# Fences on every load of the opening: banded attention followed by four experts, one core

## The chip, the cores and the metric

The kernel runs on one core of one Trainium2 chip. The metric is the device time of one execution in microseconds (us). A profile of one execution is shown beside the times; its times count from the start of its span. PE is TensorE, DVE VectorE, ACT ScalarE, POOL GpSimd, SP SyncE, whose queue issues nearly all DMAs.

## What is computed

Attention over 4 batches, 8 heads, 576 positions and 64 columns, where a query sees 32 keys at most (heads 4 to 7: every fourth key back to 128), and then a layer of 4 experts on the 2304 x 512 result, weighted by given probabilities:

```
scores = where(mask, scale * q @ k.T, -1e9)
attn = exp(scores - max); attn = attn / (sum(attn) + 1e-9)
x = (attn @ v) as 2304 x 512
p = domain_probs / (sum(domain_probs) + 1e-9)
for e in range(4):
    h = relu(x @ w1[e]); out += p[:, e] * (h @ w2[e])      # w1[e] 512x1024, w2[e] 1024x512
```

All is float32. The products of the experts are made of a high and a low part of each operand, three matmuls for one.

## The kernel before

**Attention in steps.** A step is two groups of 192 queries; there are 24. Step m goes through stages: `s_qk` (scores `sc`, 48 small matmuls, L300), `s_max` (masked maxima `sm`, `nm` on VectorE, L314), `s_sub` (GpSimd, L328), `s_exp` (ScalarE, L335), `s_sum` (row sums `su`, `rc` on VectorE, L341 to L345), `s_norm` (GpSimd, L350), `s_tr` (transpose `pt` on PE, copy `pts` on ScalarE, L361 to L365), `s_av` (products `po` with the V tile, 48 small matmuls, L381, and a copy of each of the two results to `xr`, L398 on VectorE or L400 on ScalarE).

**Experts in units.** A unit is 256 of an expert's 1024 inner columns: 16 units, each for three blocks of 768 tokens; the first two units of the first block come with attention. `fetch_w1` and `fetch_w2` load a unit's W1 (tile `r`, tag r1) and W2 (tag r2); ScalarE makes the high part and VectorE or GpSimd the low one (`split`, L127 and L130: `g1h`, `g1l`, `w2h`, `w2l`, of x `xh`, `xl`). The product with W1 is `product` (L431, results m1x, m1y), then relu (`hh`, `hl`, L449 to L455), the product with W2 is `mm2` (L535), and VectorE adds it to `acc` (L539, L544). `x_sums` (L227) are differences of x for a Strassen-like scheme.

**Rounds.** The program is written in rounds n (L851). Round n does `s_qk` of the step whose place is n, `s_max` and the later stages of the steps before; `s_av` of a step comes 3 rounds after its `s_qk`. Steps 0 to 4 have places 0 to 4, steps 5 to 9 have 8 to 12, step 10 has 16. START is 7, OPEN is 15. From round START on, pieces of the experts are taken between the stages; up to START, PE is given dummy matmuls (`wt`, L775). So `po` of step 4 is in round 7, of step 8 in round 14; `sc` of step 9 is in round 12.

**Loads.** At the start of each round, and in rounds 3 and 4 once more behind `s_max` (mid = 1), `load_ready` goes down the list `loads` and issues what is ready. A load goes to SP's queue, which is worked off in order, so a load that waits holds all behind it. A buffer's reuse makes a load wait by itself (`QKB` 3 buffers for q and k, `VB` 4 for V, 2 for W1, 1 for raw W2). A fence is a memset of one column of the tile on VectorE ahead of its DMA: the DMA waits for the memset, and the memset stands in VectorE's order where the round begins. In the kernel before, fences stand on W1 of units 0 and 2, on q of steps 5 and 10, and on V of steps 2, 3 and 4:

```
ready["w1"] = lambda u: n >= (needed[0] + 1, 0, OPEN - 2)[u]
waits = {needed[0] + 1: needed[0] + 1, needed[1] + 1: OPEN}
fenced = range(2, needed[0] + 1)
```

(needed is 4 and 9.) The rest of the opening's loads go as soon as the list and the buffers let them.

Of the kernel before, what the change touches and what calls it, by code (L numbers as in the profile page):

```python
# [23 lines left out]
QKB = 3  # L24
VB = 4
# [23 lines left out]
def kernel(  # L49
# [11 lines left out]
    nc = tc.nc  # L61
# [37 lines left out]
    w2_op = {}  # L99
    raw1 = {}  # L100
    raw2 = {}

    def fetch_w1(u, part=0):
        e, s = divmod(u % NU, FPE)
        if not part:
            raw1[u] = wp.tile([128, 4, FU], F32, tag="r1", name="r1", bufs=2)
            if u in (0, 2):
                nc.vector.memset(raw1[u][:, 0, :1], 0.0)
        c = slice(part, 4 if u or part else 2)
        src = w1[e, :, s * FU:(s + 1) * FU].rearrange("(c p) f -> p c f", p=128)  # L110
        nc.sync.dma_start(out=raw1[u][:, c], in_=src[:, c])

    def fetch_w2(u):
        e, s = divmod(u % NU, FPE)
        r = wp.tile([128, 2, DM], F32, tag="r2", name="r2")
        nc.sync.dma_start(
            out=r, in_=w2[e, s * FU:(s + 1) * FU, :].rearrange("(c p) d -> p c d", p=128)
        )
        raw2[u] = r
# [124 lines left out]
    def attention(ap, xrp, pa):  # L244
# [125 lines left out]
        def s_av(n, gs):  # L370
            ts_ = st.pop(n)
            v_s = v_of.pop(n)
            po = [pa.tile([128, 512], F32, tag="pa", name="po") for _ in gs]
            for i in range(GS):
                for half in range(2):
                    for k in range(len(gs)):
                        rows = slice(KB * k, KB * (k + 1))
                        for j in range(2):
                            c = i * 128 + 64 * (j ^ k) + QB * half
                            o = i * SB + QB * half  # L380
                            nc.tensor.matmul(  # L381
                                po[k][64 * j:64 * j + 64, o:o + QB],
                                v_s[rows, j, 2 * i + half, :], ts_[rows, c:c + QB],
                                start=True, stop=True,
                            )

            for k, (b, p, gi) in enumerate(gs):
                x = x_raw(b)[:, p, :]
                src = po[k][:, :GW]
                if p < NP // 2:  # L390
                    nt = GW // DILATION
                    dst = x.rearrange("q (r t) -> q r t", r=DILATION)
                    dst = dst[:, :, gi * nt:(gi + 1) * nt]
                    src = src.rearrange("q (t r) -> q r t", r=DILATION)
                else:
                    dst = x[:, gi * GW:(gi + 1) * GW]
                if 0 < n < 3:
                    nc.vector.tensor_copy(out=dst, in_=src)  # L398
                else:
                    nc.scalar.activation(out=dst, in_=src, func=AF.Copy)  # L400
# [258 lines left out]
    with tc.manual_schedule():  # L659
# [15 lines left out]
        s_av, s_tr, s_max = (stages[0][i][0] for i in (1, 2, 3))  # L675
# [112 lines left out]
        START = done(*dil(0, 0, 2))  # L788
        OPEN = done(*dil(1, 0))
        when = {}  # L790
        for n, i, names in (
# [8 lines left out]
        first_x = []  # L800
        qk_done = av_done = 0
        shares = []
        ready = {"w2": lambda u: u < 1 or (u - 1, 1) in w2_op and (u < 2 or n >= OPEN)}
        ready["w1"] = lambda u: n >= (needed[0] + 1, 0, OPEN - 2)[u]
        waits = {needed[0] + 1: needed[0] + 1, needed[1] + 1: OPEN}
        ready["qk"] = lambda m: m < qk_done + QKB and n >= waits.get(m, 0)
        fenced = range(2, needed[0] + 1)
        ready["v"] = lambda m: (
            m < av_done + VB
            and (m <= needed[1] or m <= qk_done)  # L810
            and (m not in fenced or (n, mid) >= ((3, 1), (4, 1))[m > 3])
        )

        def load(what, m):
            if what == "qk":
                load_qk(steps[m], nc.sync if m else nc.scalar, m in waits)
            elif what == "v":
                load_v(m, steps[m], m in fenced)
            elif what == "masks":
                load_masks()  # L820
            elif what == "rest":
                fetch_w1(m, 2)
            elif what == "probs":
                shares.append(load_probs())
            else:
                (fetch_w1 if what == "w1" else fetch_w2)(m)

        loads = [
# [4 lines left out]
        ]  # L833
        for m in range(needed[1] + 1, len(steps)):
            loads += [("qk", m), ("v", m)]
# [2 lines left out]
        def load_ready():  # L838
            at = 0
            while at < len(loads):  # L840
                what, m = loads[at]
                if ready.get(what, lambda m: True)(m):
                    load(*loads.pop(at))
                elif what == "w2" or m > needed[1]:
                    at += 1
                else:
                    break
# [3 lines left out]
        for n in range(at(len(steps) - 1) + 5):  # L851
            mid = 0
            load_ready()
            if START <= n < OPEN:
                due = len(held)
                holding.add(n)
                if START < n < OPEN - 2:
                    step()
            else:
                flush()  # L860
                holding.clear()
                due = 0
            early_order = {4: 3, 5: 3, START - 1: 4}.get(n, START + 1 < n < OPEN - 2)
            for k, order in enumerate((stages[early_order], stages[2])):
                for stage, after in order:
                    m = step_at.get(n - after, -1)
                    if m >= 0 and k == (m > needed[1]):
                        if stage is None:
                            next(ffn)
                            continue  # L870
                        if n == 2 and stage == s_tr:
                            dummies(512, 384)
                        stage(m, steps[m])
                        if n in (3, 4) and stage == s_max:
                            mid = 1
                            load_ready()
                        av_done += stage == s_av
            behind, held[:] = held[due:], held[:due]
            flush()
            held[:] = behind  # L880
            if n in step_at:
                qk_done += 1
            for i, names in when.get(n, ()):
                for name in names:
                    of = first_x if i < 2 else later
                    if name is None or name == "T2":
                        prepare(x_sums, i, of=of)
                    if name is not None:
                        prepare(x_part, i, name.upper(), of=of)
            place = 0 if n <= START or n >= OPEN else len(queue)  # L890
            queue[place:place] = first_x
            first_x.clear()
            if n == 6:
                prepare(w1_split, 0)
            if n == START:
                prepare(w2_late, 0)
            if n == START + 1:
                weigh(shares[0])
                prepare(w1_split, 1)
            if n == START + 3:  # L900
                prepare(w2_late, 1, soon=True)
            if n == OPEN:
                gate.add("open")
            if n < START:
                dummies(*((384,), (384,), (384,), (), (256,), (), (128,))[n])
                step()
                if n > 4:
                    step()
                    step()
                continue  # L910
            if "open" not in gate:
                for _ in range(2 if n < START + 2 else 1):
                    if next(ffn) == "idle":
                        dummies(256)
                step()
                if n >= OPEN - 2:
                    step()
                continue
            if n == OPEN:
                dummies(512)  # L920
            for _ in range(PACE if n in step_at else 4):
                full = next(ffn)
                step()
                if not full:
                    if n <= OPEN + 1:
                        step()
                    if len(queue) > 8:
                        step()
                    elif len(queue) < 5:
                        step(later)  # L930
# [62 lines left out]
```

## Time and profile before

| | us |
|---|---|
| median of 3 timed runs (lowest, highest) | 830.09 (829.39, 830.98) |
| the profiled execution, its own time | 833.04 |
| its span, first to last instruction | 831.3 |
| PE busy / weight loads busy | 818.6 / 724.8 |
| DVE / ACT / POOL busy | 488.9 / 316.6 / 390.9 |
| DMA | 59.15 MB, mean 71 GB/s |
| mean granted clock of PE | 0.996 |

Shares of busy time are means over the opening (attention's first steps, up to about 63 us), a middle part in which attention runs beside the experts, and a rest that is all experts. The chain that ended last is 92% PE. An idle time of an engine says what ended it; "issue" is a wait for nothing that the profile shows.

### The profile page before, as it was taken

To read this page: it belongs to the slowest core of one execution; us is meant where nothing else is said; L and a number is where in the kernel's file an instruction comes from. 1 tells how busy PE (TensorE), PEld (TensorE's weight loads), DVE (VectorE), ACT (ScalarE), POOL (GpSimd) and SP (SyncE) were. 2 spreads that over 40 slices of the span, in tenths; PEclk is the share of its full clock that TensorE was granted. 3 is DMA by queue.
4 is the path that set the end of the run, shared out by engine and by line. 5 is a ranking of instruction groups with operands and counts; after the bars stand their busy time and mean duration, and the time that the engine had idled before them with its cause. 6 is when DMAs were issued, how large, how long until landed. Compare 5 with 4: busy or idle time off the path is not lost.

```text
span 831.3 us, 15444 instructions
## 1 busy us (share of the span) xinstructions
PE 818.6 (98%) x6164; PEld 724.8 (87%) x6164; DVE 488.9 (59%) x1055; ACT 316.6 (38%) x749; POOL 390.9 (47%) x465
## 2 busy tenths in 40 slices
PE   8999999999999999999999999999999999999998
PEld 5778888888888888988988988988988988988987
DVE  5678667656775578555555555555555555555555
ACT  3445444544455445332332332332332332332321
POOL 4335878977677689452252252252252252252210
PEclk9899999999999999999999999999999999999999
DMA  7852523434322113210010010010010010010003
GB/s 217 258 174 72 173 72 92 131 117 133 118 85 72 51 52 115 89 50 27 26 51 26 27 47 29 26 51 27 27 50 26 26 51 26 26 52 1 1 26 126
DMA packets 46770, 59.15 MB, mean 71 GB/s; under 512 B 2905, under 2 KB 36313, under 8 KB 46699
## 3 DMA queue, kind: packets, MB, share of 16 engines
q1 hardware_dynamic: 46283, 57.75, 21.9%
q8 instruction: 48, 0.79, 0.4%
q10 hardware_dynamic: 416, 0.43, 0.1%
q14 instruction: 23, 0.19, 0.1%
HBM read 53.45 MB, written 4.72 MB: 70 GB/s over the span
## 4 chain that ended last, share of the span: by engine, by line
PE 92%; DVE 4%; ACT 1%; issue 1%; DMA 1%; POOL 0%; SPq 0%; POOLq 0%; DVEq 0%; ACTq 0%
PE m L535 46%; PE m1y L431 23%; PE m1x L431 18%; PE sc L300 2%; PE po L381 2%; DVE xr L227 1%; PE wt L775 1%; PE pt L361 1%; DVE acc L544 1%; DMA k_s<-kT 1%; ACT hh L449 0%; POOL sm L350 0%; DVE su L341 0%; DVE sm L314 0%; DVE s L491 0%
## 5 line engine op out<-in xcount | busy, mean ns | idle before, releaser
L544 DVE SCALAR_TENSOR_TENSOR acc<-m,pn,acc 128x512 f32<-128x512 f32 (+1 forms) x271 | 202.0, 747 | 131.4 <-PE m L535 131.2
L535 PE MATMUL m<-w2h,hh 128*128 128x512 f32 x578 | 227.3, 393 | 1.0 <-DVE acc L544 1.0
L535 PE MATMUL m<-w2l,hh 128*128 128x512 f32 x578 | 225.5, 390 | 0.0
L127 POOL TENSOR_TENSOR g2l<-r,g2h 128x256 fp32r<-128x256 f32 x116 | 86.9, 776 | 235.7 <-PE m L535 212.6
L535 PE MATMUL m<-w2h,hl 128*128 128x512 f32 x578 | 178.5, 390 | 0.0
L449 ACT ACTIVATE hh<-s 128x384 fp32r<-128x384 f32 x92 | 48.4, 526 | 238.4 <-DVE s L472 187.6
L535 PEld LDWEIGHTS m<-w2h,hl 128*128 128x128 f32 x578 | 108.3, 188 | 23.6
L535 PEld LDWEIGHTS m<-w2h,hh 128*128 128x128 f32 x578 | 108.5, 188 | 22.6 <-DVE acc L544 2.6
L535 PEld LDWEIGHTS m<-w2l,hh 128*128 128x128 f32 x578 | 108.6, 188 | 19.6
L127 POOL TENSOR_TENSOR g1l<-r,g1h 128x256 fp32r<-128x256 f32 x93 | 69.7, 770 | 67.5 <-ACT g1h L130 67.5
L127 POOL TENSOR_TENSOR w2l<-r,w2h 128x512 fp32r<-128x512 f32 x58 | 75.6, 1321 | 45.7 <-ACT w2h L130 45.4
L491 DVE TENSOR_TENSOR s<-m1y,s 128x384 f32<-128x384 f32 x46 | 25.6, 557 | 100.1 <-PE m1y L431 98.3
L482 ACT ACTIVATE u<-m1y 128x384 f32<-128x384 f32 x46 | 22.6, 492 | 144.7 <-PE m1y L431 144.7
L455 DVE SCALAR_TENSOR_TENSOR hl<-s,hh 128x384 fp32r<-128x384 f32 x92 | 55.7, 605 | 27.3 <-ACT hh L449 27.2
L431 PE MATMUL m1y<-xh_T,g2h 128*128 128x384 f32 x152 | 51.4, 338 | 0.0
L431 PE MATMUL m1y<-xl_T,g2h 128*128 128x384 f32 x152 | 51.2, 337 | 0.0
L431 PE MATMUL m1y<-xh_T,g2l 128*128 128x384 f32 x152 | 51.0, 336 | 0.0
L130 ACT ACTIVATE g2h<-r 128x256 fp32r<-128x256 f32 x120 | 41.9, 406 | 0.8 <-POOL r L168 0.8
L431 PE MATMUL m1x<-xl_B,g2h 128*128 128x384 f32 x124 | 41.7, 336 | 0.0
L431 PE MATMUL m1x<-xh_B,g2h 128*128 128x384 f32 x124 | 41.5, 335 | 0.0
L431 PE MATMUL m1x<-xh_B,g2l 128*128 128x384 f32 x124 | 41.4, 334 | 0.0
L130 ACT ACTIVATE w2h<-r 128x512 fp32r<-128x512 f32 x64 | 38.3, 621 | 0.8 <-DMA r<-w 0.8
(133 smaller groups left out, 1492.9 us busy)
## 6 DMA issues: line engine op xcount, KB each, us to landing
r<-w SPq DMA_DIRECT2D x63, 512.0 KB, 3.4
v_s<-vw SPq DMA_DIRECT2D x48, 192.0 KB, 4.5
k_s<-kT SPq DMA_DIRECT2D x23, 224.0 KB, 4.3
q_s<-qT SPq DMA_DIRECT2D x24, 192.0 KB, 4.1
out<-acc SPq DMA_DIRECT2D x17, 256.0 KB, 2.0
r<-w SPq DMA_DIRECT2D x2, 256.0 KB, 6.0
out<-acc SPq DMA_DIRECT2D x2, 128.0 KB, 1.9
k_s<-kT ACTq DMA_DIRECT2D x1, 224.0 KB, 3.6
```

What stands on the lines that cost most here:

```text
L127: lo_eng.tensor_tensor(out=lo, in0=src, in1=hi.bitcast(F32), op=ALU.subtract)
L130: nc.scalar.activation(out=hi, in_=src, func=AF.Copy)
L227: nc.vector.tensor_tensor(out=quarter(i, d), in0=quarter(i, a), in1=quarter(i, b), op=ALU.subtract)
L300: nc.tensor.matmul(banks[swap][o:o + QB, i * KB:(i + 1) * KB], q_s[h, c0:c0 + QB], k_s[h, c0:c0 + KB], start=True, stop=True, skip_group_c ...
L381: nc.tensor.matmul(po[k][64 * j:64 * j + 64, o:o + QB], v_s[rows, j, 2 * i + half, :], ts_[rows, c:c + QB], start=True, stop=True,)
L431: nc.tensor.matmul(bank, w[:, k], x[:, k], start=(first and k == 0 and i == 0), stop=(last and k == 1 and i == 2), skip_group_check=True,)
L449: nc.scalar.activation(out=hi, in_=src, func=AF.Relu)
L455: nc.vector.scalar_tensor_tensor(out=lo, in0=src, scalar=0.0, in1=hi.bitcast(F32), op0=ALU.max, op1=ALU.subtract)
L482: nc.scalar.activation(out=u2, in_=x, func=AF.Copy)
L491: nc.vector.tensor_tensor(out=s5, in0=x, in1=s5, op=ALU.add)
L535: nc.tensor.matmul(po, h, w[:, d], start=(n == 0 and x == 0), stop=(n == 3))
L544: nc.vector.scalar_tensor_tensor(out=acc[:, d], in0=po, scalar=pn[:, tt, e:e + 1], in1=acc[:, d], op0=ALU.mult, op1=ALU.add,)
```

## The change

A table `held_to` gives for 13 loads of the opening the round (and mid) before which they aren't issued, and each of these gets a fence. W1 and W2 loads take a fence like the others. W1 of unit 0, q of step 5 lose theirs and follow V of step 4 in the queue. The list of loads is put in another order from q of step 7 on. Copies of `po` go to VectorE for steps 1 to 3, before for steps 1 and 2. The mid point is taken in round 3 alone. The dummy of round 6 has 256 columns instead of 128.

```diff
-            if u in (0, 2):
+            if fence:
                 nc.vector.memset(raw1[u][:, 0, :1], 0.0)
...
-    def fetch_w2(u):
+    def fetch_w2(u, fence=False):
...
+        if fence:
+            nc.vector.memset(r[:, 0, :1], 0.0)
...
-                if 0 < n < 3:
+                if 0 < n < 4:
                     nc.vector.tensor_copy(out=dst, in_=src)
...
-        ready = {"w2": lambda u: u < 1 or (u - 1, 1) in w2_op and (u < 2 or n >= OPEN)}
-        ready["w1"] = lambda u: n >= (needed[0] + 1, 0, OPEN - 2)[u]
-        waits = {needed[0] + 1: needed[0] + 1, needed[1] + 1: OPEN}
-        ready["qk"] = lambda m: m < qk_done + QKB and n >= waits.get(m, 0)
-        fenced = range(2, needed[0] + 1)
-        ready["v"] = lambda m: (
-            m < av_done + VB
-            and (m <= needed[1] or m <= qk_done)
-            and (m not in fenced or (n, mid) >= ((3, 1), (4, 1))[m > 3])
-        )
+        held_to = {
+            ("v", 2): (3, 0), ("v", 3): (3, 1), ("v", 4): (5, 0), ("w2", 0): (START - 1, 0),
+            ("qk", 7): (START + 1, 0), ("v", 5): (START + 2, 0), ("w2", 1): (START + 3, 0),
+            ("qk", 9): (START + 4, 0), ("v", 7): (START + 5, 0), ("v", 8): (START + 6, 0),
+            ("w1", 2): (OPEN - 1, 0), ("qk", 10): (OPEN, 0), ("w2", 2): (OPEN, 0),
+        }
+        ready = {"w2": lambda u: u < 1 or (u - 1, 1) in w2_op}
+        ready["qk"] = lambda m: m < qk_done + QKB and (m <= needed[1] or n >= OPEN)
+        ready["v"] = lambda m: m < av_done + VB and (m <= needed[1] or m <= qk_done and n >= OPEN)
...
-            ("w2", 0), ("qk", 6), ("w1", 1), ("qk", 7), ("v", 5), ("qk", 8), ("qk", 9),
-            ("w2", 1), ("v", 6), ("v", 7), ("v", 8), ("v", 9), ("w1", 2),
+            ("w2", 0), ("qk", 6), ("qk", 7), ("w1", 1), ("v", 5), ("qk", 8), ("w2", 1), ("v", 6),
+            ("qk", 9), ("v", 7), ("v", 8), ("v", 9), ("w1", 2),
...
-                if ready.get(what, lambda m: True)(m):
+                start = held_to.get((what, m), (0, 0))
+                if (n, mid) >= start and ready.get(what, lambda m: True)(m):
                     load(*loads.pop(at))
-                elif what == "w2" or m > needed[1]:
+                elif m > needed[1] or (what, m) == ("w2", 2):
                     at += 1
...
-                        if n in (3, 4) and stage == s_max:
+                        if n == 3 and stage == s_max:
...
-                dummies(*((384,), (384,), (384,), (), (256,), (), (128,))[n])
+                dummies(*((384,), (384,), (384,), (), (256,), (), (256,))[n])
```

Three places show where the fences come to stand. The first is VectorE's order from the copies of step 2 to the first maxima of step 5 (`sm_631` before, `sm_628` now), before:

```order
L398 COPY xr_317<-po_465 128x4x48
L127 TENSOR_TENSOR xl_B11_0_499<-xr_317,xh_B11_0_498 128x2x192
L127 TENSOR_TENSOR g1l_541<-r1_432,g1h_540 128x256
L127 TENSOR_TENSOR hl12_545<-r1_432,hh12_544 128x256
L127 TENSOR_TENSOR g1l_541<-r1_432,g1h_540 128x256
L127 TENSOR_TENSOR xl_B21_0_579<-xr_317,xh_B21_0_578 128x2x192
L127 TENSOR_TENSOR g1l_541<-r1_432,g1h_540 128x256
L127 TENSOR_TENSOR w2l_587<-r2_443,w2h_586 128x512
L314 ISA sm_631,nm_632<-sc_605,mask_95 128x64
```

and with the change:

```order
L129 TENSOR_TENSOR xl_B11_0_482<-xr_321,xh_B11_0_481 128x2x192
L117 MEMSET r2_487 128x1
L400 COPY xr_321<-po_500 128x192
L400 COPY xr_321<-po_501 128x192
L129 TENSOR_TENSOR g1l_531<-r1_432,g1h_530 128x256
L129 TENSOR_TENSOR hl12_535<-r1_432,hh12_534 128x256
L129 TENSOR_TENSOR g1l_531<-r1_432,g1h_530 128x256
L129 TENSOR_TENSOR xl_B21_0_569<-xr_321,xh_B21_0_568 128x2x192
L129 TENSOR_TENSOR g1l_531<-r1_432,g1h_530 128x256
L129 TENSOR_TENSOR w2l_577<-r2_487,w2h_576 128x512
L275 MEMSET q_s_595 128x1
L316 ISA sm_628,nm_629<-sc_602,mask_95 128x64
```

The fence of W2 of unit 0 (`r2_487`) and the copies of step 3 have come in behind xl of the first block, the fence of q of step 7 (`q_s_595`) ahead of the maxima of step 5.

The second is VectorE's order in rounds 10 and 11, around the low parts of W2 of unit 1, before:

```order
L341 TENSOR_REDUCE su_794<-sm_708 128x6
L342 TENSOR_TENSOR su_794<-su_794,eps_68 128x6
L345 RECIPROCAL rc_795<-su_794 128x6
L539 TENSOR_SCALAR acc_0_725<-m2_801,pn_72 128x512
L127 TENSOR_TENSOR w2l_819<-r2_748,w2h_818 128x512 x2
L314 ISA sm_886,nm_887<-sc_832,mask_95 128x64
```

and with the change:

```order
L344 TENSOR_TENSOR su_786<-su_786,eps_68 128x6
L347 RECIPROCAL rc_787<-su_786 128x6
L541 TENSOR_SCALAR acc_0_726<-m2_793,pn_72 128x512
L129 TENSOR_TENSOR w2l_811<-r2_745,w2h_810 128x512 x2
L275 MEMSET q_s_824 128x1
L316 ISA sm_883,nm_884<-sc_829,mask_95 128x64
```

The fence of q of step 9 (`q_s_824`) stands behind the two w2l. The fence of that W2 itself stands one round earlier, behind the first two `acc` (L541) and ahead of the maxima of step 7.

The third is VectorE's order where round 13 begins, before:

```order
L455 SCALAR_TENSOR_TENSOR hl_1011<-m1y_825,hh_1009 128x384
L544 SCALAR_TENSOR_TENSOR acc_0_725<-m2_1022,pn_72,acc_0_725 128x512
L227 TENSOR_TENSOR xr_317<-xr_317 128x2x192
L108 MEMSET r1_1031 128x1
L341 TENSOR_REDUCE su_1079<-sm_988 128x6
```

and with the change:

```order
L457 SCALAR_TENSOR_TENSOR hl_1009<-m1y_817,hh_1007 128x384
L546 SCALAR_TENSOR_TENSOR acc_0_726<-m2_1020,pn_72,acc_0_726 128x512
L229 TENSOR_TENSOR xr_321<-xr_321 128x2x192
L285 MEMSET v_s_1029 128x1
L343 TENSOR_REDUCE su_1070<-sm_986 128x6
```

Where the fence of W1 of unit 2 stood (`r1_1031`), that of V of step 8 stands now (`v_s_1029`).

## Rows read from the trace of the kernel before

**Rows 1.** The page's 40 slices: busy tenths of PE, and its granted clock.

```profile
PE   8999999999999999999999999999999999999998
PEclk9899999999999999999999999999999999999999
```

**Rows 2.** Three windows: us, length, busy us and instructions by engine, PEclk, DMA share, GB/s.

```profile
19.50:22.90 3.40, 2.03 (x55) 1.59 (x56) 1.15 (x2) 2.16 (x6) 1.24 (x2) 1.00 1.05 264
22.90:29.70 6.80, 6.11 (x90) 5.60 (x90) 3.18 (x6) 3.74 (x10) 1.01 (x1) 0.50 1.01 339
...
43.40:46.80 3.40, 2.23 (x90) 1.73 (x92) 2.61 (x18) 1.95 (x5) 1.66 (x2) 1.00 0.39 120
```

**Rows 3.** Timeline of PE: start, us, instruction, idle before it and releaser.

```profile
21.52 0.30 PE L381 MATMUL po<-pts,v_s 64*64 64x32 f32 x2
23.59 1.62 PE L381 MATMUL po<-pts,v_s 64*64 64x32 f32 x46 [1.77 <-issue]
...
44.31 0.41 PE L300 MATMUL sc<-k_s,q_s 64*32 64x64 f32 x21
45.89 0.44 PE L300 MATMUL sc<-k_s,q_s 64*32 64x64 f32 x27 [1.17 <-issue]
```

**Rows 4.** DMA from 21.0 to 22.2 us, by queue: packets, MB, share.

```profile
q8 instruction: 1, 0.02, 5.0%
```

**Rows 5.** Timelines of VectorE and ScalarE, 17 to 31 us.

```profile
17.73 0.06 DVE L108 MEMSET r<- 128x1 f32 x1
...
18.98 0.62 DVE L398 COPY xr<-po 128x192 f32<-128x192 f32 x2 [0.22 <-PE po L381]
20.95 1.05 DVE L127 TENSOR_TENSOR xl_B<-xr,xh_B 128x384 fp32r<-128x384 f32 x1 [1.34 <-ACT xh_B L130]
...
27.44 1.14 ACT L130 ACTIVATE w2h<-r 128x512 fp32r<-128x512 f32 x2
...
28.59 0.68 DVE L127 TENSOR_TENSOR w2l<-r,w2h 128x512 fp32r<-128x512 f32 x1
30.13 0.23 DVE L314 CUSTOM_DVE_ANT_0 sm<-sc,mask 128x64 f32<-128x64 f32 x1 [0.86 <-PE sc L300]
```

**Rows 6.** Timelines of VectorE and ScalarE, 36 to 44 us.

```profile
36.40 1.37 DVE L539 TENSOR_SCALAR acc<-m,pn 128x512 f32<-128x512 f32 x2
...
41.00 1.15 ACT L130 ACTIVATE w2h<-r 128x512 fp32r<-128x512 f32 x2 [0.79 <-DMA r<-w]
...
41.67 1.75 DVE L127 TENSOR_TENSOR w2l<-r,w2h 128x512 fp32r<-128x512 f32 x2 [1.14 <-ACT w2h L130]
```

**Rows 7.** Timelines of VectorE and PE, 50 to 55 us.

```profile
50.91 1.32 DVE L227 TENSOR_TENSOR xr<-xr 128x384 f32<-128x384 f32 x1
...
52.18 0.06 DVE L108 MEMSET r<- 128x1 f32 x1
...
52.82 0.90 PE L381 MATMUL po<-pts,v_s 64*64 64x32 f32 x48
54.22 0.55 PE L361 MATMUL pt<-ident,sm 128*128 128x128 f32 x3 [0.50 <-POOL sm L350]
```

**Rows 8.** DMAs issued at 14.0, 14.5, 34.1, 92.6, 20.5: us to landing last.

```profile
v_s<-vw SPq DMA_DIRECT2D x1, 192.0 KB, 3.1
...
v_s<-vw SPq DMA_DIRECT2D x1, 192.0 KB, 3.4
...
k_s<-kT SPq DMA_DIRECT2D x1, 224.0 KB, 2.7
...
r<-w SPq DMA_DIRECT2D x1, 512.0 KB, 3.2
...
r<-w SPq DMA_DIRECT2D x1, 512.0 KB, 6.4
```

**Rows 9.** Step 10: the DMA of k issued at 57.8, and PE.

```profile
k_s<-kT SPq DMA_DIRECT2D x1, 224.0 KB, 5.0
...
62.93 0.71 PE L300 MATMUL sc<-k_s,q_s 64*32 64x64 f32 x48 [0.21 <-DMA k_s<-kT]
```

More of the change, by code (lines that the diff above doesn't have):

```diff
@@ L101, with fetch_w1 @@
     raw2 = {}
-    def fetch_w1(u, part=0):
+    def fetch_w1(u, part=0, fence=False):
         e, s = divmod(u % NU, FPE)
@@ L802 @@
         shares = []
-        ready = {"w2": lambda u: u < 1 or (u - 1, 1) in w2_op and (u < 2 or n >= OPEN)}
-        ready["w1"] = lambda u: n >= (needed[0] + 1, 0, OPEN - 2)[u]
-        waits = {needed[0] + 1: needed[0] + 1, needed[1] + 1: OPEN}
-        ready["qk"] = lambda m: m < qk_done + QKB and n >= waits.get(m, 0)
-        fenced = range(2, needed[0] + 1)
-        ready["v"] = lambda m: (
-            m < av_done + VB
-            and (m <= needed[1] or m <= qk_done)
-            and (m not in fenced or (n, mid) >= ((3, 1), (4, 1))[m > 3])
-        )
+        held_to = {
[7 more added lines that the diff above has]
+        ready["v"] = lambda m: m < av_done + VB and (m <= needed[1] or m <= qk_done and n >= OPEN)
         def load(what, m):
+            fence = (what, m) in held_to
             if what == "qk":
-                load_qk(steps[m], nc.sync if m else nc.scalar, m in waits)
+                load_qk(steps[m], nc.sync if m else nc.scalar, fence)
             elif what == "v":
-                load_v(m, steps[m], m in fenced)
+                load_v(m, steps[m], fence)
             elif what == "masks":
@@ L825, in load @@
             else:
-                (fetch_w1 if what == "w1" else fetch_w2)(m)
+                (fetch_w1 if what == "w1" else fetch_w2)(m, fence=fence)
         loads = [
```

## The prediction

> **What bounds the kernel now.** I read the page's slices first. TensorE (PE) shows 9 or more tenths in nearly every slice and a full clock but for one digit [rows 1]: outside the opening there is next to nothing for a load to win, so the change is worth what it does to the stretch up to some 63 us. All times below are on the clock of the run before, from the span's start; step m and round n are counted as in the text on the kernel.
>
> Second, the windows of that stretch. From 19.5 to 22.9 us PE is busy 2.03 of 3.40 us with the DMA engines at 1.05; then, from 22.9 to 29.7, the granted clock is 0.50, the lower of its two levels (1.2 GHz), with the DMA still at 1.01 [rows 2]. What PE did before it fell: it stood for 1.77 us in the middle of the products po of step 4 (2 issued, then a gap, then 46) [rows 3]. A second gap, 1.17 us, lies inside the scores sc of step 9, after 21 of 48; there the clock did not fall (1.00 in the window around it) [rows 2, 3]. Neither gap has a semaphore behind it that the profile names. Between the two restarts a count of the weight loads, matmuls and semaphore instructions gives 768, three times 256, and before both a packet of the instruction queue (0.02 MB) sat among the loads; [rows 4] is that of the first. So I read both gaps as PE waiting for its next block of code, which came late because the DMA queues were full. The Trainium skill ("Runtime: NRT & Kernel Launch", section "Instruction fetch mechanics") also has code in blocks of 16 KB, 256 instructions, but calls the cost of passing one mostly hidden; these gaps disagree. By that rule alone the second gap would not be code and would stay, and the sum below would be 1.2 us higher.
>
> Third, VectorE and ScalarE, since a fence is a one-column memset in VectorE's order: the load behind it starts when VectorE gets there, not when PE reaches the round.
>
> **The change part by part.**
>
> *The first tile: a gain.* The fence of the V tile of step 4 moves from behind the maxima of round 4 to behind the copies of step 1, where the memset at 17.73 stands [rows 5]. It still has the 3.4 us that such a load takes in an empty queue [rows 8] before PE wants it at 21.5. W1 and step 5 are queued behind it as before, but W2 of unit 0 now waits for the end of xl_B, 20.95 + 1.05 = 22.0 [rows 5]. With fewer loads ahead of PE's code the 1.77 us gap goes. How far that carries is not up to PE: VectorE takes the maxima of step 5 only after the first w2l, and everything to the first expert tile hangs on those maxima, which start at 30.13, then because PE at half clock was late [rows 5]. Now: W2 lands, half of a w2h pair (1.14/2 = 0.57), a w2l (0.68). A 512 KB load took 3.2 us in an empty queue and 6.4 us in a full one [rows 8]: maxima at 22.0 + 3.2 + 1.25 = 26.5 or 22.0 + 6.4 + 1.25 = 29.7, a gain of 3.6 or 0.4. The queue is then half full (V, half of W1, two tiles of step 5 within 4 us), so I take the middle, 4.8 us: maxima at 28.0, **gain 2.1 us**. That the lower clock level goes is inside this, since the same chain ends both.
>
> *Step 9, round 12: a loss.* W2 of unit 1, so far issued as soon as its buffer was free, is now fenced to round 10, behind the two acc that end at 36.40 + 1.37 = 37.8 [rows 6]. In a near empty queue it lands 3.2 us later, at 41.0, which is where ScalarE got it before (w2h at 41.00). But q and k of step 9, issued before 34.2 so far (k's row in [rows 8]), now have their fence behind the two w2l of that tile, which end at 41.67 + 1.75 = 43.4 [rows 6]. Two issues of some 0.45 us and k's 2.7 us [rows 8]: k lands at 46.6. PE comes to sc of step 9 at 44.31 and before finished it at 45.89 + 0.44 = 46.33, code gap included [rows 3]. Now it starts at 46.75, waits 2.4 us instead of 1.17, and ends at 47.4: **loss 1.1 us**. If W2 took the 6.4 us, 3.2 more; if VectorE came earlier by as much, none.
>
> *Step 8, round 14: a loss.* V of step 8, so far issued when its buffer was free, is now fenced to round 13. VectorE reaches that round at the memset of 52.18, behind an accumulation and the difference xr (50.91, 1.32) [rows 7]. PE wants the tile at 52.82 [rows 7], 0.64 us later. The first half, issued at 52.26, lands 3.1 us on; the second, 0.58 later, takes 3.4: 56.2 [rows 8]. Of the 48 matmuls po, 2 go at 55.4, the rest from 56.35 to 57.15, and the transpose pt behind them, at 54.22 before (of which 0.50 was waiting for GpSimd) [rows 7], starts at 57.15: **loss 2.9 us**. With k's 2.7 us as the nearest shorter row it is 2.2, with another 1 us in the queue 3.9. V of step 9 follows at once and lands by 57.7, before PE's next po at about 59. V of step 7, fenced to round 12 and needed in round 13, has its lead lengthened by what PE waits for step 9; I cost it at nothing. The Trainium skill ("DMA: Bandwidth & Descriptors", section "Anatomy of one DMA — SWDGE (gpsimd) path") gives a fixed part of about 2.0 us and the bytes by 436 GB/s, for DMAs that GpSimd issues; for 192 KB that is an estimate of 2.45 us, where the rows have 3.1 and 3.4. By it this loss would be 2.0, and the sum 0.9 lower: even so it speaks against holding a load to 0.64 us before its use.
>
> *Step 10, round 16: a small gain.* Its k landed after 5 us behind other loads and held sc by 0.21 us [rows 9]. Its fence stays behind the accumulations of round 14, late like PE by 2.9 us, but nothing of later steps is ahead of it now. PE has 24 products of m1 and a dummy in front. **Gain 0.2 us.**
>
> *The clock: a loss.* PE stands at po of step 8 from 52.9 to 56.35, but for 2 matmuls: 3.4 us. After 1.77 us it fell, around 1.17 it did not [rows 2, 3]; so I expect it to fall here. A full stretch like that of 22.9 to 29.7 costs half its 6.8 us, 3.4; part of it lies in the wait itself, and none is the other end. I take the middle: **loss 1.7 us**. For the 2.4 us wait at step 9 I count none, and put it in the range.
>
> *The rest.* Six more memsets of 0.06 us [rows 5] lie between waits of VectorE. The two copies of step 3 (0.62 us on VectorE, as those of step 2 [rows 5]) run from xl_B's end at 22.0, while g1l still waits for the first W1: fence at 17.7, two issues of V, 3.2 us and a g1h make 22.3 at best. If that cover is gone they cost 0.6. The dummy of 256 instead of 128 columns adds some 0.1 us ahead of po of step 4, which waits for its V tile until about 21.8 anyway (17.8 + 0.58 + 3.4). W1 and W2 of unit 2 are needed first by the splits of unit 2, after the two tiles' second half: nothing.
>
> *Sum:* -2.1 + 1.1 + 2.9 - 0.2 + 1.7 = +3.4 us. The profiled execution took 833.04 us (span 831.3), 2.95 above the median of the three timed ones, 830.09; the opening is the same program there, so I put the difference on the median: **833.5 us**.
>
> **The rivals.**
> 1. *The fences cost nothing*, the other side. If VectorE ran further ahead of PE than the rows say, by 3.9 us instead of 0.64 at round 13 and by 3.2 instead of 0.9 at round 12, both loads would land in time. Then 2.1 + 1.17 (the second code gap) + 0.2 are won: 830.1 - 3.5 = 826.6. It decides at the memset of round 13: with the load issued at 49 instead of 52.3 us. For it: PE's own delays at step 9 give other engines time. Against: the memset stands behind an accumulation that waits for PE's product, so it can't run ahead.
> 2. *Gain and waits cancel.* W2 of unit 0 lands in 3.2 us (gain 3.6), and the clock holds: -3.6 + 1.1 + 2.9 - 0.2 = +0.2, 830.3. For it: the page shows the clock full everywhere else. Against: the queue is not empty at 22.
> 3. *It does not do what it says.* Loads without a fence (the second part of W1, the weights of the experts' mix, step 6) still run behind the fenced ones in the one queue; if they fill it again, code and W2 are as late as before, and the first gain is nil: +5.5, 835.6. For it: W2's 6.4 us in that very place. Against: step 6 and W1 of unit 1 now come after W2's fence and are not in flight there.
>
> **How the numbers follow.** Forecast 0.48, rivals 0.17, 0.20 and 0.15 in that order. The forecast's own range is 831.8 (the sum without the clock's 1.7) to 836.9 (gain 0.4, clock 3.4). The range of 8 in 10 takes in rivals 2 and 3 and the edge of rival 1: 828.3 to 837.5. A measurement of this kernel tells about 0.2% (1.7 us) from no change. Faster by more than that is rival 1 and a hundredth of the rest: 0.18; within it rival 2: 0.20; slower the forecast and rival 3: 0.62.
>
> **What would show it.** Right: no gap in po of step 4 and a full clock from 22.9 to 29.7; sc of step 9 waiting for the DMA of k some 2.4 us; po of step 8 waiting some 3.4 us for v_s, with its memset less than 1 us ahead of PE; a clock of 0.50 after it. Wrong: no wait on v_s at step 8, or a memset there 3 us and more ahead of PE (rival 1); the maxima of step 5 before 27 us (rival 2); a gap in po of step 4 as before (rival 3).

## The result, and the profile after

| | before | after |
|---|---|---|
| median (lowest, highest) of 4 runs each, us | 830.44 (829.39, 830.98) | 841.2 (840.17, 842.65) |
| ratio, 95% interval | | 1.0132 [1.0111, 1.0154] |
| the profiled execution, its own time | 833.04 | 840.17 |
| its span | 831.3 | 838.4 |
| mean granted clock of it | 0.996 | 0.996 |

The change loses 10.8 us; 833.5 was forecast, with a range to 837.5. The loss lies in the opening, as the start of step 10 below shows. In the page's slices of after, PE has its low digits there, as in [rows 1], and they are lower:

```profile
PE   8869999999999999999999999999999999999998
PEclk9989999999999999999999999999999999999999
```

The timeline of PE in after, from po of step 4 to sc of step 10 (start, us, instruction, idle before it and releaser; line numbers are 2 above those of before):

```profile
22.05 0.30 PE L383 MATMUL po<-pts,v_s 64*64 64x32 f32 x2
22.57 1.22 PE L383 MATMUL po<-pts,v_s 64*64 64x32 f32 x46 [0.22 <-issue]
...
33.10 0.50 PE L537 MATMUL m<-w2h,hh 128*128 128x512 f32 x1 [1.57 <-ACT hh L451]
...
43.90 0.52 PE L363 MATMUL pt<-ident,sm 128*128 128x128 f32 x3 [1.20 <-ACT xr L402]
47.78 0.71 PE L302 MATMUL sc<-k_s,q_s 64*32 64x64 f32 x48 [2.32 <-DVE v_s L285]
...
57.74 0.42 PE L383 MATMUL po<-pts,v_s 64*64 64x32 f32 x4 [2.54 <-DMA v_s<-vw]
58.52 1.49 PE L383 MATMUL po<-pts,v_s 64*64 64x32 f32 x44 [0.36 <-DMA v_s<-vw]
59.95 0.90 PE L363 MATMUL pt<-ident,sm 128*128 128x128 f32 x3
...
70.28 0.72 PE L302 MATMUL sc<-k_s,q_s 64*32 64x64 f32 x48
```

Three waits stand there that [rows 3] and [rows 7] don't have: pt of step 6 (1.20 us, for ScalarE), sc of step 9 (2.32 us, put down to a memset of V of step 7 that ends just before; its own k, issued at 44.84, had taken 2.7 us and landed at 47.5), and po of step 8 (2.54 and 0.36 us, for its V). The gap of 1.77 us in po of step 4 [rows 3] is down to 0.22. Step 10 begins at 70.28, in [rows 9] at 62.93: 7.35 us later, and the spans differ by 7.1.

Two windows of after, in the columns of [rows 2]:

```profile
22.90:29.70 6.80, 6.11 (x115) 5.09 (x116) 3.02 (x6) 3.82 (x10) 1.01 (x1) 1.00 0.68 204
...
57.40:64.20 6.80, 6.11 (x89) 4.93 (x93) 0.82 (x4) 1.46 (x4) 1.00 (x1) 0.50 0.49 137
```

In this execution the lower clock level has left the first tile [rows 2] and comes behind po of step 8 instead, for 6.8 us as before.

VectorE and ScalarE in after, to set beside [rows 5 to 7]:

```profile
22.29 0.06 DVE L117 MEMSET r<- 128x1 f32 x1
...
37.45 0.06 DVE L117 MEMSET r<- 128x1 f32 x1
...
44.29 0.06 DVE L275 MEMSET q_s<- 128x1 f32 x1
...
54.39 0.06 DVE L285 MEMSET v_s<- 128x1 f32 x1
...
28.59 1.15 ACT L132 ACTIVATE w2h<-r 128x512 fp32r<-128x512 f32 x2 [0.63 <-DMA r<-w]
...
36.52 0.42 ACT L132 ACTIVATE g1h<-r 128x256 fp32r<-128x256 f32 x1 [3.10 <-DMA r<-w]
...
42.38 1.15 ACT L132 ACTIVATE w2h<-r 128x512 fp32r<-128x512 f32 x2 [2.44 <-DMA r<-w]
43.44 0.53 ACT L402 ACTIVATE xr<-po 128x192 f32<-128x192 f32 x2
```

The four memsets shown are the fences of W2 of unit 0, W2 of unit 1, q of step 9 and V of step 8. The last is 0.8 us ahead of PE, which had come to po of step 8 at 55.2 (57.74 less 2.54). The last two rows are the wait that was not forecast: ScalarE stands 2.44 us for W2 of unit 1, and the copies of step 5 to `xr`, behind it in ScalarE's order, free the bank that pt of step 6 needs (sc, pt and po share four banks, tag pa). The first load of W2 took 6.1 us from issue to landing, that of unit 1 4.8 us:

```profile
r<-w SPq DMA_DIRECT2D x1, 512.0 KB, 6.1
...
r<-w SPq DMA_DIRECT2D x1, 512.0 KB, 4.8
```

### The profile page after: what moved, and what is told of

The parts are those of the page before. It is cut to its first block, busy times and chain, and to the rows that moved or that the text cites. A ratio compares the mean times of both kernels' runs of the same rounds, so it can differ in the third digit from the quotient of the medians.

```text
span 838.4 us, 15454 instructions
## 1 busy us (share of the span) xinstructions
PE 820.2 (98%) x6164; PEld 724.7 (86%) x6164; DVE 489.9 (58%) x1063; ACT 316.2 (38%) x747; POOL 390.0 (47%) x465
## 2 busy tenths in 40 slices
DMA packets 46770, 59.15 MB, mean 71 GB/s; under 512 B 2905, under 2 KB 36313, under 8 KB 46699
## 4 chain that ended last, share of the span: by engine, by line
PE 91%; DVE 4%; DMA 2%; ACT 2%; issue 1%; POOL 0%; SPq 0%; POOLq 0%; ACTq 0%; DVEq 0%
PE m L537 45%; PE m1y L433 23%; PE m1x L433 17%; DMA r<-w 2%; PE po L383 2%; PE sc L302 2%; DVE xr L229 1%; PE wt L777 1%; PE pt L363 1%; DVE acc L546 1%; ACT hh L451 0%; DMA v_s<-vw 0%; DVE xl_B L129 0%; DVE hl L457 0%; DVE s L493 0%
```

## The experiments

Each was timed in five rounds beside the kernel before on the same chip; a ratio is to those runs. The kernel before took 830.4 to 831.2 us by the median there, so kernels of different groups are better compared by their ratios. The theories are named in the expectations. Diffs are against the kernel named.

**The kernel before once more** (no edit).

> The kernel before, unchanged, to see how its executions lie. Theory A (the profile of before that the sum was made on had a fall of the clock at 22.9 us that its timed runs mostly lack): runs with a mean granted clock of 1.00 near 830.4 us, and any with 0.996 near 833. Rival: every execution has the fall (clock 0.996 in all), and the 2.6 us between the first profiled execution and the median come from something else.

Measured: 830.62, ratio 0.9998 [0.9986, 1.0009]. This time the profiled execution took 829.14 us, the least of the twelve. Its slices have no low digit of the clock, the gap in po of step 4 is 0.69 us and not 1.77, and sc of step 9 has none [rows 3]:

```profile
PEclk9999999999999999999999999999999999999999
...
21.84 1.01 PE L381 MATMUL po<-pts,v_s 64*64 64x32 f32 x46 [0.69 <-issue]
30.81 0.50 PE L535 MATMUL m<-w2h,hh 128*128 128x512 f32 x1 [1.27 <-ACT hh L449]
...
40.23 0.49 PE L361 MATMUL pt<-ident,sm 128*128 128x128 f32 x3
41.69 0.72 PE L300 MATMUL sc<-k_s,q_s 64*32 64x64 f32 x48
...
49.14 0.90 PE L381 MATMUL po<-pts,v_s 64*64 64x32 f32 x48
...
59.15 0.71 PE L300 MATMUL sc<-k_s,q_s 64*32 64x64 f32 x48 [0.54 <-DMA k_s<-kT]
```

The maxima of step 5 start at 27.59 in it, and ScalarE takes W2 of unit 1 at 37.55 without a wait:

```profile
27.59 0.21 DVE L314 CUSTOM_DVE_ANT_0 sm<-sc,mask 128x64 f32<-128x64 f32 x1
...
37.55 1.14 ACT L130 ACTIVATE w2h<-r 128x512 fp32r<-128x512 f32 x2
```

So the execution of [rows 2] and [rows 5], with its fall of the clock and maxima at 30.13, was not a typical one: it took 2.6 us more than the median of 830.44. Theory A holds in kind: four of the twelve runs have a mean clock of 0.996 or less and took 831.14 to 832.00 us, the other eight 829.14 to 831.54. By the medians that is 1.3 us, less than the 2.6 it named.

Against this execution after is 2.3 us late at the first product with W2, 3.7 at pt of step 6, 6.1 at sc of step 9, 8.6 at po of step 8 and 11.1 at sc of step 10 (70.28 to 59.15). The last is about the measured loss; both executions are 1.0 to 1.5 us shorter than their kernel's median. ScalarE's 3.10 us for W1 of unit 1 in after cost PE nothing: pt of step 5 comes behind it, at 38.40 to 36.10 here, and is still 2.3 us late.

**Holds taken out, V of step 8 and q of step 9.** Three kernels, against the changed one: the first line of the diff alone, the second alone, and both. In each diff of this kind only the entries of `held_to` that go are shown.

```diff
-            ("v", 8): (START + 6, 0),
-            ("qk", 9): (START + 4, 0),
```

> The changed kernel without the hold and the fence on V of step 8. Theory A (po of step 8 waits 2.9 us for it, and the clock falls in that wait, some 2 us more): 841.2 - 5 = 836, no wait on v_s in po of step 8, clock full from 57 to 63 us. Rival (the clock falls anyway, on the wait at step 9): 841.2 - 2.9 = 838.3.

Measured: 836.14, ratio 1.0070 [1.0050, 1.0090], theory A's time. PE waits no longer at po of step 8, and still at the two places ahead of it. Now po of step 7 also waits, 0.63 us for its V, which is held too (0.37 us in v8_q9_free):

```profile
43.94 0.52 PE L363 MATMUL pt<-ident,sm 128*128 128x128 f32 x3 [1.77 <-ACT xr L402]
47.90 0.71 PE L302 MATMUL sc<-k_s,q_s 64*32 64x64 f32 x48 [2.39 <-DVE v_s L285]
...
53.33 0.89 PE L383 MATMUL po<-pts,v_s 64*64 64x32 f32 x44 [0.63 <-DMA v_s<-vw]
...
56.01 0.90 PE L383 MATMUL po<-pts,v_s 64*64 64x32 f32 x48
```

> The changed kernel without the hold and the fence on q and k of step 9. Theory A: the wait of 2.32 us at sc of step 9 goes, the fall of the clock at step 8 stays: 841.2 - 2.3 = 838.9. Rival (the wait only moves: V of step 8's fence hangs on the same VectorE chain, which is late because W2 of unit 1 is): 840.5 or more.

Measured: 841.06 (836.13 to 842.3), ratio 1.0103 [1.0076, 1.0131]. By the median nothing is won, by the ratio 2.4 us (0.0029 of 831, with overlapping intervals); the runs spread over 6 us, and the profiled one has a fall of the clock at the first tile. Alone it doesn't decide.

> Both holds taken away. Theory A (the parts add): 841.2 - 5 - 2.3 = 834, what is left over 830.4 being W2's waits at units 0 and 1 (some 1.2 at the transpose of step 6, some 1.6 at the first tile). Rival (one of the two waits hides the other): 836 or more.

Measured: 835.14, ratio 1.0053 [1.0035, 1.0071], between the two forecasts. With V of step 8 free, q of step 9 is worth 1.0 us by the medians and 1.4 by the ratios (the two intervals overlap). sc of step 9 waits for nothing, pt of step 6 still 1.95 us. The two holds carry 6.1 us by the medians, 6.6 by the ratios; some 4 are left over.

**Where the other 4 us are.** First I took the late W2 of unit 1 for the cause, then that of unit 0; each kernel takes out more of the table. First, with V of step 8 and q of step 9 free already:

```diff
-            ("w2", 1): (START + 3, 0),
```

> The changed kernel without the holds and fences of V of step 8, q of step 9 and W2 of unit 1. Theory A, each hold costs the wait that its row shows: the transposes pt of step 6 waited 1.20 to 1.95 us for ScalarE, whose copies stood behind the late w2h of unit 1; without the hold they go, and 835.1 becomes 833.3. Theory B, the waits only hand one to the next: what PE does not lose at pt of step 6 it loses at the next load, and the time stays at 835 or above.

Measured: 835.07, ratio 1.0047 [1.0029, 1.0065]: nothing won, theory A fails. W2 of unit 1 was issued at 37.72 us all the same. The wait at pt of step 6 was shorter in the profiled execution, and the time was not:

```profile
46.16 0.52 PE L363 MATMUL pt<-ident,sm 128*128 128x128 f32 x3 [0.65 <-ACT xr L402]
```

Then two more:

```diff
-            ("w2", 0): (START - 1, 0), ("v", 7): (START + 5, 0),
```

> The same, and W2 of unit 0 and V of step 7 free too. Theory A: the first product with W2 began at 33.10 us in the changed kernel and at 30.81 in an execution of the kernel before without a clock fall, 2.3 us apart, and W2 of unit 0 was issued at 22.4 and took 6.1 us; freed, the time is 831.0, that of the kernel before within 0.1%. Theory C, the rest of the change (the list's order, the copies on VectorE, V of step 4, the dummy) has a price of its own: 833 or above.

Measured: 834.99, ratio 1.0053 [1.0037, 1.0069]: nothing won again. That is theory C's time, but seven_free below shows that its reason is wrong. pt of step 6 waits 2.13 us, and SyncE's queue says why (start, us of the issue):

```profile
31.13 0.37 SPq L277 DMA_DIRECT2D q_s<-qT  x1
31.55 0.48 SPq L278 DMA_DIRECT2D k_s<-kT  x1
32.06 0.47 SPq L111 DMA_DIRECT2D r<-w  x1
35.86 1.19 SPq L287 DMA_DIRECT2D v_s<-vw  x2
37.14 0.53 SPq L277 DMA_DIRECT2D q_s<-qT  x1
37.72 0.43 SPq L278 DMA_DIRECT2D k_s<-kT  x1
38.25 0.41 SPq L118 DMA_DIRECT2D r<-w  x1
```

The queue stands until 31.1 for the fence of q of step 7, and from 32.5 to 35.9 for that of V of step 5. Neither tile is late itself; behind them are W1 (L111) and W2 (L118) of unit 1. In the kernel before (the second execution) the same W2 went at 30.58:

```profile
30.58 0.41 SPq L116 DMA_DIRECT2D r<-w  x1
```

So these two were taken out too:

```diff
-            ("qk", 7): (START + 1, 0), ("v", 5): (START + 2, 0),
```

> The changed kernel without seven of its holds: V of steps 5, 7 and 8, q of steps 7 and 9, both W2. What is left of the change is the list's order, the hold of V of step 4, the copies on VectorE and the dummy. Theory F, the hold of V of step 5 (and that of q of step 7 before it) keeps W1 and W2 of unit 1 waiting behind it in the one queue, which five_free still had: W2 of unit 1 is issued before 35 us and not at 38, pt of step 6 waits for nothing, 831.0. Theory C, the rest of the change costs the 4 us that five_free still lost: 834.5 or above.

Measured: 831.14, ratio 1.0009 [1.0000, 1.0018]: 3.7 us won by the ratios (0.0044 of 831), theory F. W2 of unit 1 goes at 33.06 and lands before ScalarE wants it, and pt of step 6 waits for nothing. ScalarE and PE:

```profile
41.46 1.14 ACT L132 ACTIVATE w2h<-r 128x512 fp32r<-128x512 f32 x2
43.10 0.55 ACT L402 ACTIVATE xr<-po 128x192 f32<-128x192 f32 x2 [0.51 <-PE po L383]
...
44.17 0.49 PE L363 MATMUL pt<-ident,sm 128*128 128x128 f32 x3
```

What is left of the change (the list, six holds, that of V of step 4 among them, copies, dummy) costs 0 to 1.5 us.

**Single parts put into the kernel before.** Four kernels, against the kernel before; in each the list waits behind the held load. V of step 8:

```diff
+            and (m != 8 or n >= START + 6)
...
-                load_v(m, steps[m], m in fenced)
+                load_v(m, steps[m], m in fenced or m == 8)
```

> The kernel before, with one part of the change: V of step 8 held to round 13 and fenced, V of step 9 and W1 of unit 2 behind it. Theory A: po of step 8 waits for v_s some 3 us, 833.5 if the clock holds and 835.5 if it falls behind the wait. Theory E: with the other loads early, VectorE reaches the fence well ahead of PE and the wait is under 1.2 us: 831.8 or below.

Measured: 834.14, ratio 1.0040 [1.0025, 1.0056], 3.3 us: theory A with the clock held. Its PE rows at po of step 8 (the first wait is put down to a VectorE row; the first half of V, issued at 48.50, took 3.1 us and landed at 51.6):

```profile
51.74 0.30 PE L381 MATMUL po<-pts,v_s 64*64 64x32 f32 x4 [1.96 <-DVE xr L227]
52.48 1.38 PE L381 MATMUL po<-pts,v_s 64*64 64x32 f32 x44 [0.44 <-DMA v_s<-vw]
```

V of step 5, by the same lines:

```diff
+            and (m != 5 or n >= START + 2)
...
-                load_v(m, steps[m], m in fenced)
+                load_v(m, steps[m], m in fenced or m == 5)
```

> The kernel before, with one part of the change: V of step 5 held to round 9 and fenced. Theory F: the tile itself is in time, but q of step 8 and W2 of unit 1 come behind it, W2 is issued some 3 to 6 us later than at 30.6, lands after 41, and pt of step 6 waits 1 to 2.5 us for ScalarE's copies behind w2h: 832 to 833.5. Theory G, only several holds together are late: 831.3 or below, no wait at pt of step 6.

Measured: 836.44, ratio 1.0065 [1.0048, 1.0083], 5.4 us: more than theory F had. V went at 33.79, W2 of unit 1 at 37.22. ScalarE and PE:

```profile
44.66 1.15 ACT L130 ACTIVATE w2h<-r 128x512 fp32r<-128x512 f32 x2 [5.11 <-DMA r<-w]
...
46.17 0.87 PE L361 MATMUL pt<-ident,sm 128*128 128x128 f32 x3 [3.86 <-ACT xr L400]
```

q of step 7:

```diff
-        waits = {needed[0] + 1: needed[0] + 1, needed[1] + 1: OPEN}
+        waits = {needed[0] + 1: needed[0] + 1, needed[1] + 1: OPEN, 7: START + 1}
...
-            ("w2", 0), ("qk", 6), ("w1", 1), ("qk", 7),
+            ("w2", 0), ("qk", 6), ("qk", 7), ("w1", 1),
```

> The kernel before, with one part of the change: q of step 7 held to round 8 and fenced, and put ahead of W1 of unit 1 in the list. Theory F: W1 of unit 1 comes at 31 us instead of 24 to 25, all behind it later by as much, W2 of unit 1 lands near 41 and pt of step 6 waits up to 1.5 us: 831.5 to 832.8. Theory G: W1 of unit 1 is not needed before 36 us, and the rest has lead enough: 831.3 or below.

Measured: 835.16, ratio 1.0062 [1.0042, 1.0082], 5.1 us, again above theory F: pt of step 6 waits 2.32 us for the copies. Either hold alone makes the wait. They don't add: taken out together above, they were worth 3.7 us.

W2 of unit 0, with the fence of the changed `fetch_w2`:

```diff
-        ready = {"w2": lambda u: u < 1 or (u - 1, 1) in w2_op and (u < 2 or n >= OPEN)}
+        ready = {"w2": lambda u: u < 1 and n >= START - 1 or (u - 1, 1) in w2_op and (u < 2 or n >= OPEN)}
...
-                (fetch_w1 if what == "w1" else fetch_w2)(m)
+                fetch_w1(m) if what == "w1" else fetch_w2(m, not m)
...
-                elif what == "w2" or m > needed[1]:
+                elif what == "w2" and m or m > needed[1]:
```

> The kernel before, with one part of the change: W2 of unit 0 held to round 6 and fenced, and what follows it in the list waiting behind it. Theory A: 2.3 us above the kernel before, 832.9, and the first product with W2 about 33 us into the span. Theory D, my forecast's, that with fewer loads in the queue W2 lands in 3 to 5 us and the maxima of step 5 come no later: 831.4 or below.

Measured: 831.12, ratio 1.0005 [0.9994, 1.0016]: theory A's 2.3 us are not there. W2 goes at 22.27 and not at 20.84, but the first product with it begins without a wait at 32.38, where it stood 1.27 us for hh before. That start, too, lies between those of the kernel before (30.81 and 33.59).

**The other way about.** What the kernel before still waits for, against it:

```diff
-        waits = {needed[0] + 1: needed[0] + 1, needed[1] + 1: OPEN}
+        waits = {needed[0] + 1: needed[0] + 1, needed[1] + 1: OPEN - 1}
...
-            ("v", 1), ("v", 2), ("v", 3), ("v", 4), ("w1", 0), ("qk", 5), ("rest", 0), ("probs", 0),
-            ("w2", 0), ("qk", 6),
+            ("v", 1), ("v", 2), ("v", 3), ("v", 4), ("w1", 0), ("w2", 0), ("qk", 5), ("rest", 0), ("probs", 0),
+            ("qk", 6),
```

> The kernel before, the other way about: W2 of unit 0 ahead of q of step 5 in the list, and q of step 10 held to round 14 instead of 15. If the 1.27 us that the first product with W2 waited and the 0.54 us of k of step 10 are PE's own loss, 829.1 to 829.8; if q of step 5 or PE's code comes later for it, 830.8 or above.

Measured: 831.88, ratio 1.0019 [1.0007, 1.0030]. Both waits shrink (1.27 to 0.41 us, 0.54 to 0.17), but the gap in po of step 4 is 1.24 us and not 0.69, and nothing is won. That the edit made the gap longer isn't shown: in before_hold_v8 and before_hold_v5, which don't touch the loads ahead of it, it was 0.97 and 1.25. No version here beats the kernel before.

**How the parts add, with the changed kernel's other holds in place.**

> The changed kernel, unchanged, to see how its time goes with the granted clock. Theory H: its 10.8 us are some 6.4 us of waits (pt of step 6 1.2, sc of step 9 2.3, po of step 8 2.9) and the rest work at the lower level of the clock, 1 minus the mean clock times the span, 6.9 us in its first four runs and 2.1 in those of the kernel before: median 840.5 to 842, and the longer ones at the lower clock. Theory I, the waits themselves are longer than the profile shows: times with no relation to the clock.

Measured: 841.54 (841.46 to 842.21), ratio 1.0133 [1.0118, 1.0147]. The three waits are there again (1.18, 2.31, then 1.92 and 0.45 us), some 6 us. 1 minus the mean clock times the span gives 6.1 us here and 2.1 in the runs of before beside it. Waits and the added lower clock (4.0) together come to 10 of the 11 us, near theory H. But these four runs don't follow the clock: 841.58 us at 0.988, 842.21 at 0.994 (of the first four, those at 0.996 took 840.2, those at 0.987 and 0.988 842.1 and 842.7). That part of H fails, and so the near sum is no proof.

The other two, against the changed kernel, take out both lines, or the first alone:

```diff
-            ("qk", 7): (START + 1, 0), ("v", 5): (START + 2, 0),
-            ("w2", 1): (START + 3, 0),
```

> The changed kernel without the holds of q of step 7, V of step 5 and W2 of unit 1; V of steps 7 and 8, q of step 9 and W2 of unit 0 stay held. Theory F: pt of step 6 waits for nothing, the waits at sc of step 9 and po of step 8 stay; 841.2 less the 3.9 us that lie between five_free and seven_free: 837 to 838. Theory J, without that wait PE comes to the next fence earlier and waits there instead: 840 or above.

Measured: 839.2 (837.32 to 844.41), ratio 1.0106 [1.0084, 1.0128], between the two theories. W2 of unit 1 goes at 33.01 and pt of step 6 waits for nothing; sc of step 9 (1.94 us) and po of step 8 (1.81 and 0.46) wait as before.

> The same with W2 of unit 1 held to round 10 as in the changed kernel. Theory F: its own fence lies behind the two acc that end at 37.5 us, so it is issued as late as in the changed kernel and pt of step 6 waits its 1 to 2 us all the same: 840 to 841.5. Theory K, only what the queue holds in front of W2 counts: 837 to 838, as without its hold.

Measured: 840.47, ratio 1.0115 [1.0102, 1.0128]. The time is theory F's, the reason is not. W2 of unit 1 goes as late as in the changed kernel (37.72), but with no V and no q and k just ahead of it ScalarE has it at 41.62, and pt of step 6 waits 0.28 us only. It took 3.9 us, in the changed kernel 4.8. That most of the 1.20 us there came from what was in flight around W2 is a reading of this. What the runs do show: its own hold and the two ahead of it each keep W2 until 37.72 (v8_q9_w21_free and this kernel), and without all three it goes at 33.0.

## Why the prediction was wrong

1. **First tile, gain 2.1: wrong, the step that failed first.** The gain was counted from an execution in which the clock had fallen, and then put on the median: "the opening is the same program there". The program is, the execution is not. In the second execution the maxima start at 27.59, and in before_hold_v8, whose program is the same up to there, at 28.17; against these the 28.0 that I had forecast for the change is next to no gain. Nor did the change reach it: its maxima start at 29.87. Of the mechanism the code came in time (a gap of 0.22 us in po of step 4), and the clock was full to 29.7 in one profiled execution, though not in the other (0.50 from 17.2 to 30.7 us in after_again). But W2 took 6.1 us where 4.8 was taken, and against the execution that the sum was made on the gain was 0.5 us (the first product with W2 at 33.10, before at 33.59). Measured for what seven_free keeps: 0 to 1.5 us of loss.
2. **Holds on q of step 7 and V of step 5: no term at all, and that of W2 of unit 1 at nothing.** I asked of each hold whether its own tile comes in time, and not what it keeps waiting in the queue. The title's "every load" says too much: W1 of unit 1 and q and k of step 8 have no hold of their own, and wait behind these two as W2 of unit 1 does. For W2 the sentence "lands 3.2 us later, at 41.0, which is where ScalarE got it before" hid it. [rows 6] already had ScalarE waiting 0.79 us for it, so there was no slack in that execution (in the second it had gone at 30.58 and was there in time). In the changed kernel it took 4.8 us and was ready at 42.38. W2's own hold and these two hide each other, so the price depends on the order: those on q of step 7 and V of step 5 are worth 3.7 us taken out last and 5.1 and 5.4 put in alone; taken out with the other holds in place, 1.5 by the ratios (2.2 with that of W2 of unit 1), which is within the intervals.
3. **Step 9, loss 1.1: the wait right, the price in part luck.** sc waited 2.32 us (2.4 forecast), and the hold is worth 1.0 to 1.4 us between v8_free and v8_q9_free. But the 1.1 had a code gap of 1.17 us taken off, which the second execution of the kernel before doesn't have. Why a wait of this length costs only half of it, the runs don't show.
4. **Step 8, loss 2.9, and the clock, 1.7: right in kind and nearly in size.** The wait was 2.9 us (2.54 and 0.36) where 3.4 was forecast, the fence 0.8 us ahead of PE, the clock 0.50 for 6.8 us behind it. Together 4.6 were forecast; taking the hold out gives 5.2, putting it into the kernel before 3.3. What the clock alone cost was not measured.
5. **Step 10, gain 0.2: right as to the wait.** sc of step 10 waits for nothing (in the second execution of before 0.54 us); what that is worth was not measured by itself.
6. **The rest, nothing:** within the 0 to 1.5 us of seven_free. V of step 7 makes PE wait 0.63 us once V of step 8 is free; without its hold (five_free) nothing is won.

By the ratios the steps from after to seven_free are 5.2, 1.4, 0.5, -0.5 and 3.7 us, and 0.7 remain to the kernel before: 11.0 (10.8 by the medians). Only the first and the fifth are clear of their intervals. They add up because they are one chain of kernels; in another order the single sizes differ (point 2). Of the miss, 7.6 us (11.0 against 3.4), 2.8 are point 1 (2.1 of gain not had, 0.7 lost), 3.7 point 2 and the rest points 3 to 5. Rivals 1 and 2 fail with the memset at 54.39 and the maxima at 29.87. Rival 3's first gain of nil came true by half: the queue was full, with the DMA engines at 0.92 and 0.96 from 22 to 24 and 24 to 26 us, and W2 was late; but the code was in time.

The Trainium skill's estimate for V of step 8 ("DMA: Bandwidth & Descriptors", section "Anatomy of one DMA — SWDGE (gpsimd) path") was 2.45 us, from a figure for DMAs that GpSimd issues; the row, of SyncE's queue, has more:

```profile
v_s<-vw SPq DMA_DIRECT2D x2, 192.0 KB, 3.2
```

## What to carry to other kernels

In a queue that is worked off in order, a hold on one load is a hold on all that stand behind it: price it at the last of them, on the engine that consumes it and on what stands behind that consumer in its own order. Before a gain is read from a stall, look whether a second execution has the stall; a difference to one execution can't be put on a median that lies 3 us lower. A fence less than 1 us ahead of the need makes the engine wait for most of the transfer, here 2.9 us at po of step 8; what that costs in the end has to be measured, as step 9 shows (2.3 us of wait, 1.0 to 1.4 of time).

## What was not expected of the hardware

- The same kernel shows the stalls that I read as code (which no run tested) in very different size: the gap in po of step 4 was 1.77 us in one execution of the kernel before and 0.69 in another, and only behind the longer one did the clock fall. In the changed kernel a gap of the same kind, inside po of step 1, was 1.27 us in both profiled executions (0.75 and 0.72 in those of the kernel before). From its end to that of the gap in po of step 4 PE has 256 weight loads, matmuls and semaphore instructions in either kernel, which fits that reading. Behind the gap in po of step 1 the clock fell in one execution of the changed kernel (0.50 from 17.2 to 30.7 us) and not in the other. The times are 841.58 and 840.17 us, 1.4 apart for 13.5 us at half the clock. That the later waits for loads take up the rest is a reading.
- Kernels with added waits also worked more at the lower level: by 1 minus the mean clock times the span 6.9 and 6.1 us in eight runs of the changed kernel, 2.1 in twelve of the kernel before. Not all of that can be the waits' doing: seven_free, which has none of the three, had 3.3 us (1.6 in the runs beside it) and lost only 0.7, and in the profiled execution of after_again the longest stretch at the lower level lies ahead of all three waits. How much each wait brings, the runs don't tell.
